# Moving the q and k transposes of an attention-plus-MLP kernel from TensorE to DMA, with a new order of the first batch

## The chip, the cores and the metric

The kernel runs on one NeuronCore of one Trainium2 chip. The metric is the device time of one execution in microseconds (us), as the median of several executions. The profile is one traced execution, and its span runs from the first instruction to the last, about 2 us less than the timed figure.

Engines are named as in the profile: PE is TensorE, PEld its weight loads, DVE is VectorE, ACT is ScalarE, POOL is GpSimd and SP is SyncE. "SPq" is the sequencer of SP while it issues DMAs. SP does nothing else here, and it works through its instructions in program order.

## The reference

Attention with a forget gate, then a two-layer MLP. Cut to what matters:

```python
# q, k, v: (8, 8, 576, 64) f32; f: (8, 8, 576) f32; w_in: (512, 2048); w_out: (2048, 512)
scores = matmul(q, k^T) / 8 + cum[..., :, None] - cum[..., None, :]     # cum = cumsum(log f)
scores = where(causal, -1e9, scores)                                     # strictly above the diagonal
attn   = softmax(scores)
x = matmul(attn, v).transpose(0, 2, 1, 3).reshape(8 * 576, 512)
h = x @ w_in
out = (h * sigmoid(h)) @ w_out                                           # (4608, 512) f32
```

## The kernel before

The work is cut into 32 *units*. A unit is a pair of heads (two times 64 columns fill 128 partitions), four units make a batch. For the scores, q and k are needed with the head dimension on the partitions. They come from memory with the sequence on the partitions, so each unit transposes nine blocks of 128 x 128: four of q, four of k, and one that holds the 64-row tails of both.

The parts that the change touches, with cuts marked:

```python
def load_qk(n):            # four DMAs of 128 KB on SP, q and k, four buffers each
    ...
def cast_qk(n, engs):      # f32 -> bf16, qkb, two buffers; POOL in the steady stage
    ...
def transposes(n):
    b, p = divmod(n, NP)
    src = qbf.pop(n)
    tp = psc.tile([P, 2048], BF16, name="tp", tag="sc")                  # PSUM
    for i in range(2):
        for c in range(NM):                                              # NM = 4
            o = i * (S + ST) + c * P
            nc.tensor.transpose(tp[:, o : o + P], src[:, i, c, :], ident_bf[:, :])
    nc.tensor.transpose(tp[:, SM : SM + P], tbf[b][:, p * P : (p + 1) * P], ident_bf[:, :])
    t = qktp.tile([P, QKW], BF16, name="qkT", tag="qkT")                 # two buffers
    nc.vector.tensor_copy(out=t[:, :], in_=tp[:, 0:QKW])                 # PSUM -> SBUF on DVE
    qkT[n] = t
```

`scores(n, c)` computes a quarter of a unit's scores from `qkT` on PE and their exponentials on ACT. `den(n // 2)` makes the denominators of two units. `rec_part` inverts them on DVE and then issues eight small DMAs on SP that spread the reciprocals over the partitions (`rb`). `num(n)` multiplies by v, with `vp` being v times the gate's weights, made on POOL. It then multiplies by `rb` into `xT`, the input of the MLP.

The MLP is cut into 288 *chunks* of four matmuls, either of the first layer (`hp`) or of the second (`po`). `fill(k)` puts up to k chunks that are ready into PE's program, between the attention's matmuls. What isn't put in earlier is done after the last unit.

```python
cast_qk(0, (nc.vector, nc.gpsimd)); cast_tails(0); transposes(0)
for n in range(NU):
    b, p = divmod(n, NP)
    scores(n, 0); scores(n, 1); fill(1)
    if n + 1 < NU: cast_qk(n + 1, (nc.gpsimd, nc.gpsimd))
    if n + 4 < NU: load_qk(n + 4)
    if n == 2:                                    # v of the first batch, then w_in, on POOL
        for c in range(NM + 1): convert_v(0, c)
        for i in range(WQ): load_w_in(i)
    ...                                           # w_out at unit 5; next batch's v: loads at p == 0,
    ...                                           # products at p == 2 and 3
    fill(1)
    scores(n, 2); scores(n, 3)
    fill(2 if n % 2 == 0 else 1)
    if n + 1 < NU: transposes(n + 1)
    fill(2)
    if n % 2 == 1:
        den(n // 2); rec_part(n // 2, 0); fill(2); rec_part(n // 2, 1); fill(1)
    elif n >= 2:
        num(n - 2); num(n - 1); fill(2); finished(n - 1)
fill(12); num(NU - 2); fill(2); num(NU - 1); finished(NU - 1)
while fill(1): pass
```

The softmax here doesn't subtract the row's maximum and nothing guards it: scores larger than these inputs give would overflow.

## Time and profile before

Three executions gave a median of 421.75 us, from 420.9 to 421.83.

| stage (profiled run, 418.7 us) | PE busy | PE clock | DMA share |
|---|---|---|---|
| 20 to 45 us (start) | 7.0 of 25 us | 0.71 | 1.13 |
| 45 to 66 us (start) | 10.5 of 21 us | 0.58 | 0.92 |
| 142 to 310 us (units 12 to 27) | 159.0 of 168 us | 1.00 | 0.60 |

The DMA share counts whole every packet that starts in the stretch, so it can pass 1. PE clock is the granted share of full speed.

The page of the kernel before comes first. The rows of tenths give the busy share in 40 equal slices of the span, and PEclk is the granted clock in tenths.

```profile
span 418.7 us, 8037 instructions
...
PE 359.0 (86%) x3109; PEld 176.8 (42%) x3109; DVE 249.9 (60%) x406; ACT 213.2 (51%) x328; POOL 95.9 (23%) x140
...
PE   1650456989998999899989998999899989999996
...
PEclk9995565999999999999999999999999999999999
DMA  8999699761696179617861696169614021300111
...
q1 hardware_dynamic: 124944, 47.36, 50.1%
...
PE 50%; DVE 17%; SPq 11%; ACT 9%; DMA 6%; issue 5%; POOL 1%; ACTq 0%; DVEq 0%; POOLq 0%
...
L224 DVE COPY qkT<-tp 128x1152 bf16<-128x1152 bf16 x32 | 24.0, 750 | 4.2 <-PE tp L220 4.1
L219 PE MATMUL tp<-ident_bf,qkb 128*128 128x128 bf16 x256 | 21.9, 235 | 3.8 <-ACT u L254 2.9
```

PE is busy for 80% or more from slice 8 on (the last slice apart). Before that the DMA engines are busy for 60% to over 90%. The last two lines are the groups that the change removes: 288 PE transposes (256 here, 32 on the next source line) and 32 copies on DVE. The line of PE and DVE shares is the chain of waits that ended last.

The order in time of PE (start, duration, line, operation; in brackets the idle time before it and what ended it):

```profile
45.53 0.52 PE L247 MATMUL sc<-qkT 64*128 64x400 bf16 x2 [14.71 <-DVE xT L334]
...
65.32 0.52 PE L247 MATMUL sc<-qkT 64*128 64x400 bf16 x2 [5.30 <-DVE xT L334]
...
67.26 1.04 PE L352 MATMUL hp<-xT,w_in_bf 128*128 128x512 bf16 x2
...
156.20 0.61 PE L219 MATMUL tp<-ident_bf,qkb 128*128 128x128 bf16 x8 [0.20 <-ACT u L254]
156.65 0.22 PE L220 MATMUL tp<-ident_bf,qkt 128*128 128x128 bf16 x1
156.70 1.89 PE L352 MATMUL hp<-xT,w_in_bf 128*128 128x512 bf16 x8
```

Two things are read here. At the start PE stands still for 14.71 us before unit 3, until `xT` has its `rb`. In the steady stage nine transposes take 0.50 us of PE, from 156.20 to 156.70.

What held `rb` back is in the order of SP's issues:

```profile
15.69 1.15 SPq L112 DMA_DIRECT2D vf_129<-in_v_dram  x1
...
26.20 5.90 SPq L112 DMA_DIRECT2D vf_226<-in_v_dram  x1
32.16 4.12 SPq L77 DMA_DIRECT2D qf<-in_q_dram  x2
36.32 3.90 SPq L77 DMA_DIRECT2D kf<-in_k_dram  x2
40.33 5.02 SPq L312 DMA_DIRECT2D rb<-rec  x8
```

The first batch's v loads were all issued by 16.8 us. The `rb` of units 0 and 1 came at 40.33, behind loads of later units.

### The profile page before, as it was taken

The page shows a single profiled execution, that of the slowest core. Times are in us where ns is not written, and L with a number is a line of the kernel's source. Part 1 is how long each engine was busy: PE and PEld are TensorE (multiplying, and loading weights), DVE is VectorE, ACT ScalarE, POOL GpSimd, SP SyncE. Part 2 cuts the span into 40 slices and gives each one's busy share as a digit, 9 for nine tenths or more (in the row PEclk, how much of TensorE's full clock was granted, in tenths as well). Part 3 has the DMA queues.
Part 4 walks back from the last instruction along what each step waited for, and adds up shares of the span by engine and source line. Part 5 has one row for each costly group of instructions (what it writes and reads, how often), then busy time and mean ns, then how long its engine had stood idle before and what let it go on. Part 6 is the DMA issues. An engine that isn't in the chain of part 4 may idle for free.

```text
span 418.7 us, 8037 instructions
## 1 busy us (share of the span) xinstructions
PE 359.0 (86%) x3109; PEld 176.8 (42%) x3109; DVE 249.9 (60%) x406; ACT 213.2 (51%) x328; POOL 95.9 (23%) x140
## 2 busy tenths in 40 slices
PE   1650456989998999899989998999899989999996
PEld 1430232434543454345434444444444444444442
DVE  3670354976497649764976397549754964574410
ACT  3530334845484558455845484548454852463421
POOL 3682330601171116011601161116111000000000
PEclk9995565999999999999999999999999999999999
DMA  8999699761696179617861696169614021300111
GB/s 171 217 208 201 154 157 235 120 145 43 167 202 144 42 178 194 145 43 182 188 143 45 156 207 151 34 154 218 150 34 126 8 52 50 108 2 26 50 52 75
DMA packets 129206, 52.06 MB, mean 124 GB/s; under 512 B 116304, under 2 KB 120400, under 8 KB 129168
## 3 DMA queue, kind: packets, MB, share of 16 engines
q1 hardware_dynamic: 124944, 47.36, 50.1%
q0 software_dynamic: 4224, 4.19, 6.2%
q8 instruction: 24, 0.39, 0.4%
q14 instruction: 14, 0.11, 0.1%
HBM read 36.85 MB, written 9.44 MB: 111 GB/s over the span
## 4 chain that ended last, share of the span: by engine, by line
PE 50%; DVE 17%; SPq 11%; ACT 9%; DMA 6%; issue 5%; POOL 1%; ACTq 0%; DVEq 0%; POOLq 0%
PE po L379 26%; PE hp L352 14%; DVE gt L361 7%; DVE rec L304 6%; ACT u L254 6%; SPq L77 4%; SPq L312 4%; PE nm L325 3%; PE sc L247 3%; PE dn L290 2%; PE tp L219 2%; ACT th L360 2%; DMA out_dram<-osb 2%; SPq L112 1%; DVE u L261 1%
## 5 line engine op out<-in xcount | busy, mean ns | idle before, releaser
L352 PE MATMUL hp<-xT,w_in_bf 128*128 128x512 bf16 x576 | 137.6, 383 | 0.1
L379 PE MATMUL po<-w_out_bf,gt 128*128 128x512 bf16 x576 | 134.5, 380 | 0.0
L254 ACT ACTIVATE u<-sc 128x800 bf16<-128x800 f32 x128 | 101.2, 847 | 53.9 <-PE sc L247 43.9
L360 ACT ACTIVATE th<-hp 128x512 bf16<-128x512 f32 x144 | 85.0, 611 | 57.5 <-PE hp L352 53.0
L361 DVE SCALAR_TENSOR_TENSOR gt<-th,hp 128x512 bf16<-128x512 bf16 x144 | 94.1, 676 | 24.4 <-ACT th L360 23.7
L352 PEld LDWEIGHTS <-w_in_bf 128*128 128x128 bf16 x576 | 52.5, 98 | 60.9 <-issue 5.9
L379 PEld LDWEIGHTS <-gt 128*128 128x128 bf16 x576 | 52.7, 98 | 60.0 <-issue 2.0
L261 DVE TENSOR_TENSOR u<-u,mask 128x256 bf16<-128x256 bf16 x128 | 42.4, 346 | 57.7 <-ACT u L254 57.4
L247 PE MATMUL sc<-qkT 64*128 64x176 bf16 (+5 forms) x512 | 40.0, 269 | 36.2 <-DVE xT L334 20.0
L304 DVE RECIPROCAL rec<-rec 128x288 f32<-128x288 f32 x32 | 61.1, 1934 | 15.7 <-ACT rec L298 15.7
L388 ACT ACTIVATE osb<-po 128x512 f32<-128x512 f32 x36 | 21.5, 597 | 74.6 <-PE po L379 55.6
L96 POOL CAST qkb<-qf 128x512 bf16<-128x512 f32 x31 | 19.9, 643 | 142.2 <-PE tp L220 79.0
L334 DVE TENSOR_TENSOR xT<-nm,rb 128x576 bf16<-128x576 f32 x32 | 23.6, 753 | 43.5 <-DMA rb<-rec 26.7
L247 PEld LDWEIGHTS <-qkT 64*128 64x128 bf16 x512 | 20.3, 99 | 67.4 <-issue 63.0
L325 PE MATMUL nm<-u,vp 128*64 128x64 bf16 (+4 forms) x576 | 28.4, 250 | 8.4 <-DVE qkT L224 8.4
L325 PEld LDWEIGHTS <-vp 128*64 128x64 bf16 x576 | 21.0, 114 | 20.4 <-issue 15.9
L224 DVE COPY qkT<-tp 128x1152 bf16<-128x1152 bf16 x32 | 24.0, 750 | 4.2 <-PE tp L220 4.1
L219 PE MATMUL tp<-ident_bf,qkb 128*128 128x128 bf16 x256 | 21.9, 235 | 3.8 <-ACT u L254 2.9
L219 PEld LDWEIGHTS <-qkb 128*128 128x128 bf16 x256 | 18.8, 105 | 12.0 <-issue 5.2
L96 POOL CAST qkb<-kf 128x512 bf16<-128x512 f32 x32 | 20.1, 627 | 4.8 <-DMA kf<-in_k_dram 4.8
L103 POOL CAST qkt<-qktf 128x512 bf16<-128x512 f32 x8 | 4.9, 616 | 58.4 <-DMA qktf<-in_k_dram 58.4
L298 ACT ACTIVATE rec<-dn 128x576 f32<-128x576 f32 x16 | 10.4, 651 | 13.1 <-PE dn L290 12.9
(73 smaller groups left out, 112.7 us busy)
## 6 DMA issues: line engine op xcount, KB each, us to landing
rb<-rec SPq DMA_DIRECT2D x128, 72.0 KB, 2.0
out_dram<-osb SPq DMA_DIRECT2D x36, 256.0 KB, 2.3
qf<-in_q_dram SPq DMA_DIRECT2D x64, 128.0 KB, 3.1
kf<-in_k_dram SPq DMA_DIRECT2D x64, 128.0 KB, 3.0
w_in_bf<-in_moe_w_in_dram POOLq DMA_DIRECT2D x4, 512.0 KB, 11.1
w_out_bf<-in_moe_w_out_dram POOLq DMA_DIRECT2D x4, 512.0 KB, 9.9
qktf<-in_q_dram SPq DMA_DIRECT2D x8, 128.0 KB, 3.2
qktf<-in_k_dram SPq DMA_DIRECT2D x8, 128.0 KB, 3.5
```

Of the source, the lines that this page charges most:

```text
L96: engs[i].tensor_copy(out=t2[:, i, :, :], in_=t[:, :, :, :].rearrange("p c h d -> p c (h d)"))
L219: nc.tensor.transpose(tp[:, o : o + P], src[:, i, c, :], ident_bf[:, :])
L224: nc.vector.tensor_copy(out=t[:, :], in_=tp[:, 0:QKW])
L247: nc.tensor.matmul(sc[:, i, lo - c * CW : hi - c * CW], lhsT=t[r, k_off(kb) : k_off(kb) + P], rhs=t[r, q0 : q0 + hi - lo], start=True, sto ...
L254: nc.scalar.activation(out=u[:, :, c * CW : (c + 1) * CW], in_=sc[:, :, 0:CW], func=ACT.Exp, scale=scale)
L261: nc.vector.tensor_tensor(out=x, in0=x, in1=mask[:, None, :].to_broadcast([P, 2, P]), op=ALU.mult)
L304: nc.vector.reciprocal(out=rec[:, r], in_=rec[:, r])
L325: nc.tensor.matmul(nm[i * D : (i + 1) * D, q0:q1], lhsT=vp[:, kb, 2 * p + i, :], rhs=u_part(n, i, kb, q0, q1), start=(kb == 0), stop=(kb = ...
L352: nc.tensor.matmul(hp[:, :], lhsT=w_in_bf[:, cc, fc * P : (fc + 1) * P], rhs=xT[:, cc, t0 : t0 + TG], start=(cc == 0), stop=(cc == NCC - 1),)
L360: nc.scalar.activation(out=th[:, :], in_=hp[:, :], func=ACT.Tanh, scale=0.5)
L361: nc.vector.scalar_tensor_tensor(out=gt[:, fc, :], in0=th[:, :], scalar=1.0, in1=hp[:, :], op0=ALU.add, op1=ALU.mult,)
L379: nc.tensor.matmul(po[:, :], lhsT=gt[:, fc, tb * P : (tb + 1) * P], rhs=w_out_bf[:, fc, :], start=(fc == 0), stop=(fc == NFC - 1),)
```

## The change

The intent is to take 32 times nine transposes off PE and the copies off DVE. One DMA transpose per unit now goes from SBUF to SBUF, issued by SP. The first batch is put in a new order, so that PE doesn't wait for `rb` in units 0 to 3. The diff, cut to its core:

```diff
-    qktp ... bufs=2      rbp ... bufs=3      qf, kf ... bufs=4      qktf ... (1)
+    qktp ... bufs=3      rbp ... bufs=4      qf, kf ... bufs=5      qktf ... bufs=2
     def cast_qk(n, engs):                 # the tails now go into the same tile, nine blocks wide
...
     def transposes(n):
-        ...  nine nc.tensor.transpose into PSUM, one nc.vector.tensor_copy
+        t = qktp.tile([P, NX, P], BF16, name="qkT", tag="qkT")
+        nc.sync.dma_start_transpose(
+            out=t[:, :, :], in_=qbf.pop(n)[:, :, :].rearrange("p x c -> p (x c)")
+        )
+        qkT[n] = t[:, :, :].rearrange("p x c -> p (x c)")
...
-            can2 = c < 16 * (a // 16)
+            can2 = c < 16 * (a // 16) and a >= 32          # second layer only after 32 first-layer chunks
...
     transposes(0)
+    for n in range(1, NP):
+        load_qk(n + 1)
+        cast_qk(n, (nc.gpsimd, nc.gpsimd))
+        if n == NP - 1:
+            for c in range(NM + 1): load_v(0, c)
+        transposes(n)
+    for i in range(WQ): load_w_in(i)
+    for c in range(NM + 1): convert_v(0, c)
+    load_tails(1); load_qk(NP + 1)
     # unit n:
         scores(n, 0); scores(n, 1); fill(1)
-        cast_qk(n + 1), load_qk(n + 4)
+        cast_qk(n + 2), load_qk(n + 5)
-        v(b + 1): loads at p == 0, products at p == 2, 3      w_out at unit 5
+        v: loads at p == 2, products at p == 0, 1 of its own batch (b > 0)   w_out at unit 6
-        fill(1)
+        fill(1 if n >= 2 * NP else 0)                         # fewer fills in units 4 to 7
         scores(n, 2); scores(n, 3)
-        fill(2 if n % 2 == 0 else 1); transposes(n + 1); fill(2)
+        fill(4 - n % 2 if n >= 2 * NP else 1)
         den, rec_part (odd n)  /  num(n - 2), num(n - 1) (even n)
+        # num(0) to num(3) all at the end of unit 3, then fill(4)
+        if n + 2 < NU and n + 2 >= NP:
+            transposes(n + 2)                                 # at the end of the unit
+        if n + 5 < NU and 1 <= n < NP: load_qk(n + 5)
+        if n == NP - 1: load_v(1, ...)
```

Below, T(n) is the DMA transpose of unit n.

More of the change, by code (lines that the diff above doesn't have):

```diff
@@ L42 @@
     NM = SM // P
+    NX = 2 * NM + 1
     assert D == 64 and S == 576 and DM == H * D and NP == NCC
@@ L51 @@
     vpool = ctx.enter_context(tc.tile_pool(name="vpool", bufs=3))
-    qktp = ctx.enter_context(tc.tile_pool(name="qktp", bufs=2))
+    qktp = ctx.enter_context(tc.tile_pool(name="qktp", bufs=3))
     upool = ctx.enter_context(tc.tile_pool(name="upool", bufs=4))
     recp = ctx.enter_context(tc.tile_pool(name="recp", bufs=2))
-    rbp = ctx.enter_context(tc.tile_pool(name="rbp", bufs=3))
+    rbp = ctx.enter_context(tc.tile_pool(name="rbp", bufs=4))
     tpool = ctx.enter_context(tc.tile_pool(name="tpool", bufs=3))
@@ L67 @@
     qbf: dict[int, bass.AP] = {}
-    tbf: dict[int, bass.AP] = {}
     vbf: dict[int, bass.AP] = {}
@@ L74, in load_qk @@
         for name, src in (("qf", q), ("kf", k)):
-            t = stage.tile([P, NM, 2, D], FP32, name=name, tag=name, bufs=4)
+            t = stage.tile([P, NM, 2, D], FP32, name=name, tag=name, bufs=5)
             for i in range(2):
@@ L84, in load_tails @@
     def load_tails(b):
-        t = stage.tile([P, H, D], FP32, name="qktf", tag="qktf")
+        t = stage.tile([P, H, D], FP32, name="qktf", tag="qktf", bufs=2)
         for i, src in enumerate((q, k)):
@@ L93, in cast_qk @@
     def cast_qk(n, engs):
-        t2 = conv.tile([P, 2, NM, 2 * D], BF16, name="qkb", tag="qkb")
+        b, p = divmod(n, NP)
+        t2 = conv.tile([P, NX, 2 * D], BF16, name="qkb", tag="qkb")
         for i, t in enumerate(qst.pop(n)):
+            c0 = i * (NM + 1)
             engs[i].tensor_copy(
-                out=t2[:, i, :, :], in_=t[:, :, :, :].rearrange("p c h d -> p c (h d)")
-            )
+                out=t2[:, c0 : c0 + NM, :],
+                in_=t[:, :, :, :].rearrange("p c h d -> p c (h d)"),
+            )
+        nc.gpsimd.tensor_copy(
+            out=t2[:, NM, :],
+            in_=tst[b][:, 2 * p : 2 * p + 2, :].rearrange("s h d -> s (h d)"),
+        )
         qbf[n] = t2
-    def cast_tails(b):
-        t2 = conv.tile([P, H * D], BF16, name="qkt", tag="qkt")
-        nc.gpsimd.tensor_copy(out=t2[:, :], in_=tst.pop(b)[:, :, :].rearrange("s h d -> s (h d)"))
-        tbf[b] = t2
     def load_v(b, c):
@@ L120 @@
     load_tails(0)
-    for n in range(1, NP):
-        load_qk(n)
-    for c in range(NM + 1):
-        load_v(0, c)
+    load_qk(1)
     ident_bf = const.tile([P, P], BF16, name="ident_bf")
@@ L177 @@
     )
+    cast_qk(0, (nc.vector, nc.vector))
     nc.vector.tensor_copy(out=wexp[:, S : S + ST], in_=wexp[:, SM:S])
@@ L204, in convert_v @@
         )
-    QKW = 2 * S
     def k_off(kb):
@@ L212, in transposes @@
     def transposes(n):
-        b, p = divmod(n, NP)
-        src = qbf.pop(n)
-        tp = psc.tile([P, 2048], BF16, name="tp", tag="sc")
-        for i in range(2):
-            for c in range(NM):
-                o = i * (S + ST) + c * P
-                nc.tensor.transpose(tp[:, o : o + P], src[:, i, c, :], ident_bf[:, :])
-        nc.tensor.transpose(
-            tp[:, SM : SM + P], tbf[b][:, p * P : (p + 1) * P], ident_bf[:, :]
-        )
-        t = qktp.tile([P, QKW], BF16, name="qkT", tag="qkT")
-        nc.vector.tensor_copy(out=t[:, :], in_=tp[:, 0:QKW])
-        qkT[n] = t
+        t = qktp.tile([P, NX, P], BF16, name="qkT", tag="qkT")
+        nc.sync.dma_start_transpose(
+            out=t[:, :, :], in_=qbf.pop(n)[:, :, :].rearrange("p x c -> p (x c)")
+        )
+        qkT[n] = t[:, :, :].rearrange("p x c -> p (x c)")
     UO = [0]
@@ L411, in finished, with steady @@
             ready["g"] += 1
-    cast_qk(0, (nc.vector, nc.gpsimd))
-    cast_tails(0)
     transposes(0)
-    for n in range(NU):
+    for n in range(1, NP):
+        load_qk(n + 1)
+        cast_qk(n, (nc.gpsimd, nc.gpsimd))
+        if n == NP - 1:
+            for c in range(NM + 1):
+                load_v(0, c)
+        transposes(n)
+    for i in range(WQ):
+        load_w_in(i)
+    for c in range(NM + 1):
+        convert_v(0, c)
+    load_tails(1)
+    load_qk(NP + 1)
+    def steady(n):
         b, p = divmod(n, NP)
@@ L421 @@
         fill(1)
-        if n + 1 < NU:
-            cast_qk(n + 1, (nc.gpsimd, nc.gpsimd))
-        if n + 4 < NU:
-            load_qk(n + 4)
-        if n == 2:
-            for c in range(NM + 1):
-                convert_v(0, c)
-            for i in range(WQ):
-                load_w_in(i)
-        if n == 5:
+        if n + 2 < NU and n + 2 >= NP:
+            cast_qk(n + 2, (nc.gpsimd, nc.gpsimd))
+        if n + 5 < NU and n >= NP:
+            load_qk(n + 5)
+        if b + 1 < B:
+            if p == 0 and b > 0:
+                load_tails(b + 1)
+            if p == 2 and b > 0:
+                for c in range(NM + 1):
+                    load_v(b + 1, c)
+        if b > 0:
+            if p == 0:
+                for c in range(2):
+                    convert_v(b, c)
+            if p == 1:
+                for c in range(2, NM + 1):
+                    convert_v(b, c)
+        if n == NP + 2:
             for i in range(WQ):
                 load_w_out(i)
-        if b + 1 < B:
-            if p == 0:
-                load_tails(b + 1)
-                for c in range(NM + 1):
-                    load_v(b + 1, c)
-            if p == 2:
-                cast_tails(b + 1)
-                for c in range(2):
-                    convert_v(b + 1, c)
-            if p == 3:
-                for c in range(2, NM + 1):
-                    convert_v(b + 1, c)
-        fill(1)
+        fill(1 if n >= 2 * NP else 0)
         scores(n, 2)
         scores(n, 3)
-        fill(2 if n % 2 == 0 else 1)
-        if n + 1 < NU:
-            transposes(n + 1)
-        fill(2)
+        fill(4 - n % 2 if n >= 2 * NP else 1)
         if n % 2 == 1:
@@ L455 @@
             rec_part(n // 2, 0)
-            fill(2)
+            fill(2 if n >= 2 * NP else 1)
             rec_part(n // 2, 1)
-            fill(1)
-        elif n >= 2:
+            fill(1 if n >= 2 * NP else 0)
+            if n == NP - 1:
+                for m in range(NP):
+                    num(m)
+                finished(n)
+                fill(4)
+        elif n >= 2 and n != 2 and n != NP:
             num(n - 2)
             num(n - 1)
-            fill(2)
+            fill(2 if n >= 2 * NP else 1)
             finished(n - 1)
+        if n + 2 < NU and n + 2 >= NP:
+            transposes(n + 2)
+        if n + 5 < NU and 1 <= n < NP:
+            load_qk(n + 5)
+        if n == NP - 1:
+            for c in range(NM + 1):
+                load_v(1, c)
+    for n in range(NU):
+        steady(n)
     fill(12)
```

## The prediction

> **What bounds the kernel now.** Three stages, from the timeline and the busy table by stretches (unit = head pair).
>
> - Start, 0 to 100 us (units 0 to 7). Not TensorE: PE is busy 7.0 of 25 us in 20-45 at clock 0.71, 10.5 of 21 us in 45-66; the DMA share is 1.13 and 0.92. PE waits 14.7 us before 45.5 for xT, xT for rb, whose eight issues started only at 40.3, behind v and q/k issues of up to 5.9 us on the SP queue. A second such wait, 5.3 us, ends at 65.3. The first hp matmul starts at 67.3.
> - Steady, 100 to 352 us: 10.5 us per unit, PE bound (153-195: busy 39.9 of 42 us). In the chain of waits eight MLP matmuls take 1.73 us (216 ns each), so eight fills of four are 6.9 us; scores, num, den about 1.8; transposes 0.50 (156.20 to 156.70); about 1.2 are bubbles.
> - Tail, 352 to 419 us: MLP at 216 ns per matmul.
>
> **Removed.** 288 PE transposes, 0.50 us x 32 = 16 us of PE time, 12 us of it in the PE-bound stage. 32 qkT copies on DVE (24.0 us, 750 ns each); the waits show PE num 8.4 us and PE scores 4.5 us behind them: I expect 2 to 4 us from that.
>
> **Added.** 32 DMA transposes of 295 KB. Estimate: the DMA page's q1 has 124,944 packets taking 50.1% of 16 engines' span, 27 ns each; 1152 rows of 256 B over 16 engines are 1.9 us. The Trainium skill ("DMA: Bandwidth & Descriptors", Latency and other measured facts) gives DMA transposes 261 GB/s, so 1.1 us; this trace shows none. Steady DMA: 0.60 x 10.5 + 2 = 8.3 of 9.9 us per unit, tight, not binding. SP's issues at 0.5-0.6 us each are about 6.5 us per unit; I guess 2 us for a transpose, so 8.5. Two units of lead and a third qkT buffer hide its latency.
>
> **Moved.** w_in comes right after the first units' loads; num(0..3) wait for unit 3, so scores 0 to 3 don't stall on rb; v(1) and w_out come later. Unit 4 should start near 42 us, the first hp at 38-45 instead of 67. Units 4 to 7 do 3 fills each, at 7 to 9 us (DMA, SP, DVE bound), so unit 8 starts near 74 instead of 100. By then 16 fills are done instead of 24: 8 x 0.86 = 7 us return in the tail. Net start gain about 19 us.
>
> **Sum.** 74 + 24 x 9.85 (236) + tail 67 + 7 = 384 us span, about 386 us timed; range 373 to 412. Faster by over 2%: 0.82; within 2%: 0.09; slower: 0.09.
>
> **Right if** PE waits before 60 us shrink by over half; first hp near 40 us; unit pitch 9.6-10.0 us; transposes land in 2-5 us; scores wait little on qkT. **Wrong if** the pitch stays 10.5 (the transposes were in bubbles), unit 8 starts after 85, or the tail grows by over 10 us.
>
> **What would make it wrong.** A transpose that holds SP over 4 us, or moves under 100 GB/s: SP is in order, so rb, outputs and loads queue behind it and a unit takes 11 us or more. A backlog of loads at the start could delay transposes 0 to 3. A PE idle for longer at the start may run at a lower clock.

## The result and the profile after

The changed kernel took **441.02 us** (median of four executions, 438.02 to 441.99) against **421.36 us** for the kernel before in the same rounds. The ratio is 1.0455, with a 95% interval of 1.0401 to 1.0508: slower. Ratios here are the mean time of one kernel's fast runs over that of the other's of the same rounds, so they are not quite the ratio of the quoted medians.

The page after, in the lines that answer to those above:

```profile
span 436.2 us, 7419 instructions
...
PE 336.6 (77%) x2774; PEld 158.4 (36%) x2821; DVE 235.0 (54%) x375; ACT 213.2 (49%) x328; POOL 97.9 (22%) x163
...
PE   0511728608298899788988997898899899999996
...
PEclk9999859957789999999999999999999999999999
DMA  6999769899544987697598839894941413001011
...
q1 hardware_dynamic: 162832, 56.80, 61.2%
...
PE 42%; SPq 27%; DMA 18%; ACT 5%; issue 4%; DVE 2%; POOL 1%; POOLq 0%; DVEq 0%; ACTq 0%
```

PE lost 22.4 us of busy time, of which about 16 us are the transposes. A few per cent of its matmul records are missing from this trace (560 and 545 of 576 in the two MLP groups), so the rest isn't to be read. The span grew by 17.5 us although PE has less to do: PE now waits. In the chain of waits SP's sequencer and the DMAs went from 17% to 45%.

The order in time of PE after:

```profile
41.82 0.85 PE L238 MATMUL sc<-qkT 64*128 64x400 bf16 x6 [18.34 <-DMA qkT<-qkb]
...
53.97 0.63 PE L343 MATMUL hp<-xT,w_in_bf 128*128 128x512 bf16 x1 [0.33 <-issue]
60.72 0.59 PE L343 MATMUL hp<-xT,w_in_bf 128*128 128x512 bf16 x1 [6.12 <-DVE xT L325]
...
67.38 0.52 PE L238 MATMUL sc<-qkT 64*128 64x400 bf16 x6
...
97.67 0.85 PE L238 MATMUL sc<-qkT 64*128 64x400 bf16 x6 [13.85 <-DMA qkT<-qkb]
...
182.32 0.51 PE L238 MATMUL sc<-qkT 64*128 64x400 bf16 x6 [2.13 <-DMA qkT<-qkb]
...
192.37 0.52 PE L238 MATMUL sc<-qkT 64*128 64x400 bf16 x6 [1.05 <-DMA qkT<-qkb]
```

These are the starts of units 3 (41.82), 4 (67.38), 7 (97.67), 15 and 16. The old wait before unit 3 is gone in name but not in size: 18.34 us for a transposed q and k, where it was 14.71 us for `xT`. Unit 7 has a new one of 13.85 us. Units far into the steady stage wait 1 to 2 us each. The table of waits gives the sum (engine, line, what it waited for, us in total, times, longest):

```profile
PE sc L238 <- DMA qkT<-qkb: 63.5, 18, 18.3
```

SP's issues at the start and in the steady stage, after, show why:

```profile
20.66 0.51 SPq L115 DMA_DIRECT2D vf_198<-in_v_dram  x1
...
23.56 7.18 SPq L115 DMA_DIRECT2D vf_201<-in_v_dram  x1
30.79 4.43 SPq L115 DMA_DIRECT2D vf_202<-in_v_dram  x1
35.33 4.24 SPq L213 DMA_TRANSPOSE qkT<-qkb  x1
...
43.31 5.04 SPq L303 DMA_DIRECT2D rb<-rec  x8
...
50.80 1.61 SPq L213 DMA_TRANSPOSE qkT<-qkb  x1
...
55.84 4.96 SPq L303 DMA_DIRECT2D rb<-rec  x8
```

```profile
173.05 5.01 SPq L303 DMA_DIRECT2D rb<-rec  x8
178.18 2.16 SPq L213 DMA_TRANSPOSE qkT<-qkb  x1
...
188.15 1.82 SPq L213 DMA_TRANSPOSE qkT<-qkb  x1
```

At the start SP is never free from 19.56 to 62.17 us. T(3) stands behind the five v loads, the first `rb` group behind T(3) and six loads, T(4) behind four more loads, and the second `rb` group behind T(4) and another four. Each is needed by PE. In the steady stage T(15) is issued at the moment when the eight `rb` issues end, and the scores of unit 15 start 2.0 us after its issue ends. T(16) stands behind five v loads. So the transposes that were meant to be two units ahead are finished just in time or late.

The view of the transpose's own line gives issue time (min/median/max in ns) and the time to landing:

```profile
L213 SPq DMA_TRANSPOSE qkT<-qkb x32: 1256/1595/4237, 8.6 to 342.1; - x32
...
DMA to landing us min/median/max: 3.2/3.9/8.2
```

Where the time went, as start of units in us, with the number of MLP chunks that PE had done by then:

| | unit 3 | unit 4 | unit 6 | unit 8 | unit 12 | unit 28 | end |
|---|---|---|---|---|---|---|---|
| before | 45.5 | 52.4 (0) | 78.3 (8) | 100.2 (24) | 142.1 (56) | 310.3 (184) | 418.7 |
| after | 41.8 | 67.4 (4) | 77.8 (9) | 106.4 (15) | 151.8 (40) | 315.5 (168) | 436.2 |

At unit 12 the changed kernel is 9.7 us late and owes 16 chunks. A chunk is four matmuls of 216 ns, 0.864 us, so the debt is 13.8 us: together 23.5 us. From unit 12 to 28 it gains 4.5 us. I call "lateness plus debt" the **work-adjusted delay** and use it below. It compares kernels that do their MLP work at different times.

### The profile page after: what moved, and what is told of

The parts are those of the page before. It is cut to its first block, busy times and chain, and to the rows that moved or that the text cites. A ratio compares the mean times of both kernels' runs of the same rounds, so it can differ in the third digit from the quotient of the medians.

```text
span 436.2 us, 7419 instructions
## 1 busy us (share of the span) xinstructions
PE 336.6 (77%) x2774; PEld 158.4 (36%) x2821; DVE 235.0 (54%) x375; ACT 213.2 (49%) x328; POOL 97.9 (22%) x163
## 3 DMA queue, kind: packets, MB, share of 16 engines
q1 hardware_dynamic: 162832, 56.80, 61.2%
## 4 chain that ended last, share of the span: by engine, by line
PE 42%; SPq 27%; DMA 18%; ACT 5%; issue 4%; DVE 2%; POOL 1%; POOLq 0%; DVEq 0%; ACTq 0%
PE hp L343 19%; PE po L370 18%; SPq L303 11%; DMA qkT<-qkb 11%; SPq L77 6%; SPq L115 5%; SPq L213 4%; DMA vf_199<-in_v_dram 3%; ACT u L245 3%; PE sc L238 3%; DMA rb<-rec 2%; PE nm L316 2%; ACT th L351 2%; PE dn L281 1%; DMA vf_3622<-in_v_dram 1%
## 5 line engine op out<-in xcount | busy, mean ns | idle before, releaser
L343 PE MATMUL hp<-xT,w_in_bf 128*128 128x512 bf16 x560 | 141.0, 390 | 10.4 <-DVE xT L325 8.0
L370 PE MATMUL po<-w_out_bf,gt 128*128 128x512 bf16 x545 | 132.5, 379 | 3.3 <-issue 2.5
L245 ACT ACTIVATE u<-sc 128x800 bf16<-128x800 f32 x128 | 100.0, 841 | 68.1 <-PE sc L238 67.8
L252 DVE TENSOR_TENSOR u<-u,mask 128x256 bf16<-128x256 bf16 x128 | 53.2, 431 | 74.2 <-ACT u L245 73.1
L238 PE MATMUL sc<-qkT 64*128 64x176 bf16 (+5 forms) x512 | 38.9, 269 | 70.2 <-DMA qkT<-qkb 63.5
L370 PEld LDWEIGHTS <-gt 128*128 128x128 bf16 x576 | 53.8, 98 | 64.2 <-issue 2.6
L316 PEld LDWEIGHTS <-vp 128*64 128x64 bf16 x576 | 20.3, 115 | 14.9 <-issue 10.0
L281 PE MATMUL dn<-u,w_bf 128*32 128x64 bf16 (+4 forms) x576 | 15.9, 256 | 1.3 <-DVE u L252 0.9
L281 PEld LDWEIGHTS <-w_bf 128*32 128x32 bf16 x576 | 10.6, 101 | 11.5 <-issue 7.1
L103 POOL CAST qkb<-qktf 128x128 bf16<-128x128 f32 x32 | 9.7, 303 | 5.5 <-DMA qktf<-in_k_dram 5.5
L257 DVE TENSOR_TENSOR u<-u,mask_t 128x128 bf16<-128x128 bf16 x32 | 7.6, 238 | 0.0
## 6 DMA issues: line engine op xcount, KB each, us to landing
w_in_bf<-in_moe_w_in_dram POOLq DMA_DIRECT2D x4, 512.0 KB, 11.8
```

The source lines that it names most:

```text
L238: nc.tensor.matmul(sc[:, i, lo - c * CW : hi - c * CW], lhsT=t[r, k_off(kb) : k_off(kb) + P], rhs=t[r, q0 : q0 + hi - lo], start=True, sto ...
L245: nc.scalar.activation(out=u[:, :, c * CW : (c + 1) * CW], in_=sc[:, :, 0:CW], func=ACT.Exp, scale=scale)
L252: nc.vector.tensor_tensor(out=x, in0=x, in1=mask[:, None, :].to_broadcast([P, 2, P]), op=ALU.mult)
L281: nc.tensor.matmul(dn[32 * j : 32 * j + 32, q0:q1], lhsT=w_bf[:, kb, bh : bh + 1].to_broadcast([P, 32]), rhs=u_part(n, i, kb, q0, q1), sta ...
L316: nc.tensor.matmul(nm[i * D : (i + 1) * D, q0:q1], lhsT=vp[:, kb, 2 * p + i, :], rhs=u_part(n, i, kb, q0, q1), start=(kb == 0), stop=(kb = ...
L343: nc.tensor.matmul(hp[:, :], lhsT=w_in_bf[:, cc, fc * P : (fc + 1) * P], rhs=xT[:, cc, t0 : t0 + TG], start=(cc == 0), stop=(cc == NCC - 1),)
```

## The experiments

My theory after reading the traces: (a) the place of T in SP's in-order queue costs the steady stage; (b) the start is bound by DMA traffic and by SP, so neither a new order nor DMA transposes can shorten it, and the transposes add to it; (c) the fewer fills only move work into the tail. The rivals: each transpose is simply too costly (its bytes, or SP's time); or the order of v and w_in at the start is the whole fault; or the fills are. Every run below gave correct results.

| run | median us | ratio to before [95%] | unit 8 at us (chunks) | delay at unit 12 | us per unit, 12 to 28 |
|---|---|---|---|---|---|
| before | 420.7 to 421.4 | 1 | 100.2 (24) | 0 | 10.51 |
| the change | 441.02 | 1.0455 [1.0401, 1.0508] | 106.4 (15) | +23.5 | 10.23 |
| e1_early_issue | 426.09 | 1.0135 [1.0104, 1.0165] | 100.2 (15) | +16.0 | 9.88 |
| e2_start_order | 442.11 | 1.0514 [1.0477, 1.0551] | 106.5 (15) | +22.7 | 10.53 |
| e4_transposes_only | 424.27 | 1.0078 [1.0044, 1.0112] | 113.5 (24) | +12.9 | 10.15 |
| e5_reorder_only | 437.88 | 1.0412 [1.0380, 1.0445] | 93.5 (15) | +11.8 | 10.81 |
| e6_old_fills | 423.37 | 1.0033 [1.0001, 1.0064] | 113.7 (32) | +12.1 | 10.07 |
| e7_hybrid | 409.57 | 0.9712 [0.9671, 0.9753] | 98.6 (24) | -4.2 | 10.20 |
| e7b_hybrid_v_late | **405.37** | 0.9624 [0.9599, 0.9650] | 98.7 (24) | -2.9 | 9.90 |
| e8_double_transpose | 431.68 | 1.0234 [1.0211, 1.0256] | | | 11.18 |
| e9_tiny_issues | 436.17 | 1.0360 [1.0314, 1.0407] | | | 11.11 |
| e10_plain_copy_bytes | 426.08 | 1.0133 [1.0087, 1.0178] | | | 10.76 |
| e16_new_start_pe | 411.15 | 0.9758 [0.9715, 0.9802] | 102.9 (32) | +0.7 | 9.80 |
| e18_hybrid_k_on_act | 406.43 | 0.9667 [0.9641, 0.9693] | | | 9.75 |
| e19_loads_on_act | 490.07 | 1.1658 [1.1634, 1.1682] | | | 12.10 |
| e20_w_in_after_v | 437.16 | 1.0404 [1.0363, 1.0445] | 102.7 (15) | +19.0 | 10.33 |
| e21_best_w_in_after_v | 406.20 | 0.9662 [0.9626, 0.9697] | 100.3 (32) | -1.9 | 9.78 |

The profiled execution of e8 fell in the slow state (437.08 us; its other three were 430 to 432), so its 11.18 may be a little high, and so may its row in the table of SP times below.

### e1: issue each transpose right behind its casts

```diff
 # the changed kernel, unit n
         cast_qk(n + 2, (nc.gpsimd, nc.gpsimd))
+        transposes(n + 2)
...
-        if n + 2 < NU and n + 2 >= NP:
-            transposes(n + 2)           # was at the end of the unit
```

> The changed kernel, with each DMA transpose of unit n+2 issued right behind its casts at the start of unit n, instead of at the end of unit n behind the rb issues (odd units) or the v loads (even units). Theory A (late issue: the in-order SP queue puts the transpose behind rb and loads, so the lead of two units shrinks to 2 us): scores stop waiting for qkT after 110 us (under 5 us in all, against about 45), pitch of units 8 to 31 falls from 10.39 to about 9.85 us, time 422 to 428 us. Theory B (the transposes' DMA traffic itself slows everything): landings stay slow, pitch stays at 10.3 or more, time 434 or more.

It gained 14.9 us on the change. The waits of the scores for their transposed operands fell from 63.5 us in 18 places to three, and the pitch (us per unit) fell from 10.23 to 9.88, close to the 9.85 that I had predicted for the change. The expectation was for units 8 to 31, where it fell less, from 10.39 to 10.08. The table of waits of e1:

```profile
PE sc L238 <- DMA qkT<-qkb: 22.9, 3, 17.9
```

In SP's order in e1, T(16) is now ahead of the v loads and no longer behind them, and the scores of unit 16 start 9.1 us after its issue ended (it was 2.4 us). (T is L213.)

```profile
172.57 1.35 SPq L213 DMA_TRANSPOSE qkT<-qkb  x1
...
176.26 4.55 SPq L115 DMA_DIRECT2D vf<-in_v_dram  x5
```

So part (a) stands: the same transposes, with the same bytes and about the same SP time (8.34 and 8.56 us per unit), cost 15 us more in the place that the change gave them. Half of that lies before unit 12, where the delay falls by 7.5 us. The three waits that are left all end by 40.9 us. After 110 us there is none, where the change had 24.3 us of them (not the 45 that I wrote in the expectation). The kernel is still slightly slower than before.

### e2: T(3) ahead of the first batch's v loads

```diff
     for n in range(1, NP):
         load_qk(n + 1); cast_qk(n, ...)
-        if n == NP - 1:
-            for c in range(NM + 1): load_v(0, c)
         transposes(n)
+    for c in range(NM + 1): load_v(0, c)
     for i in range(WQ): load_w_in(i)
```

> The changed kernel, with the fourth transpose issued before the five loads of v of the first batch, instead of behind them. Theory A: the 18.3 us wait of TensorE before unit 3 (ends at 41.8) shrinks to under 3 us, unit 8 starts 5 to 15 us earlier than 106.4, time 425 to 434. Rival (the start is limited by the bytes of v and w_in, in whatever order): xT of unit 3 is still not ready before 60 us, unit 8 starts within 3 us of 106.4, time 436 to 441.

PE's order in time in e2, units 3 and 4:

```profile
33.28 0.85 PE L238 MATMUL sc<-qkT 64*128 64x400 bf16 x6 [10.11 <-DMA qkT<-qkb]
...
67.31 0.51 PE L238 MATMUL sc<-qkT 64*128 64x400 bf16 x6
```

Unit 3 came 8.5 us earlier, and unit 4 not at all (67.31 against 67.38). The five v issues still took SP from 22.15 to 39.16, and the `rb` group behind them started at 42.98 instead of 43.31. The rival was right here (its range for the time, 436 to 441, was missed by 1 us): T(3)'s long wait is the first thing one sees in the trace, but it isn't the one that ends last.

### e4: only the transposes swapped, in the order of before

```diff
 # the kernel before; transposes(n) is the DMA transpose, tails cast into the same tile
     cast_qk(0, ...); transposes(0)
+    cast_qk(1, ...); transposes(1)
...
-        cast_qk(n + 1, ...)                 # and transposes(n + 1) late in the unit
+        cast_qk(n + 2, ...)
+        transposes(n + 2)
```

> The kernel before with only its transposes swapped: DMA transposes two units ahead, issued right behind their casts; first batch, fills and load order as before. Theory A: pitch about 9.85 us in the steady stage, start within 5 us of before (unit 8 at 95 to 105), time 402 to 410. Theory B: pitch 10.3 or more, time 418 or more. Theory C (the reordering of the first batch and the fills alone make the change slow): this kernel is faster than before, as under A.

The first form of this, with T in the old place and one unit ahead, could not be run: its build stops with a deadlock. By the order of the program, a v load on SP waits for POOL's product of the batch before, that product stands behind a cast, the cast waits for a buffer that T frees, and T stands behind the v load on SP. So in this order the DMA transposes needed an earlier place.

As run, e4 is 0.8% slower than before, which is a miss: I had expected 402 to 410 us or, if the transposes were costly everywhere, 418 or more with a pitch of 10.3. In the steady stage it gains 0.36 us a unit. At the start the first scores begin at 21.1 instead of 11.1 us, because T(0) stands behind all the first loads on SP and is issued only at 16.9. By unit 12 it is 12.9 us late, at equal chunks. Of this, 7.0 us are left by unit 28.

### e5: only the reorder, transposes on TensorE

```diff
 # the changed kernel; transposes(n) as nine nc.tensor.transpose and a copy on DVE, in the change's place
-    qktp ... bufs=3     rbp ... bufs=4
+    qktp ... bufs=4     rbp ... bufs=3
```

> The changed kernel with its transposes back on TensorE and DVE (a fourth qkT buffer, one rb buffer less, both forced by order and space); all reordering kept. Theory A: pitch back at 10.4 to 10.5 us, start better than the changed kernel since no transpose stands in the SP queue (unit 8 at 85 to 98), tail as in the changed kernel, time 415 to 425. Theory C: unit 8 still at 103 or later, time 430 or more.

The reorder alone costs 4.1%. Here, too, my expectation failed: unit 8 came in the range of theory A, the time in that of theory C. It reaches unit 8 at 93.5 us, with 15 chunks instead of 24, so it isn't ahead, and at unit 12 it is 11.8 us behind after the debt is counted. Together with e4 this gives a small two-by-two table of the work-adjusted delay at unit 12:

| | TensorE transposes | DMA transposes |
|---|---|---|
| order of before | 0 | +12.9 (e4) |
| order of the change | +11.8 (e5) | +23.5 (the change) |

The two parts each cost about 12 us at the start. That they add up to the 23.5 us is partly luck, since the two entries hold delays that the change doesn't have. Unit 0 starts at 21.1 us in e4, where T(0) stands behind the first loads. In e5 it starts at 16.7 us, because PE's program has the transposes of units 0 to 3 ahead of unit 0's scores. In the change it starts at 12.1 us, in the kernel before at 11.1. A cleaner pair is e6 and e16 below. The pitch of e5, 10.81, is worse than that of before. Its PE transposes stand at the end of a unit, but v, the fills and the buffers differ too, so the cause of that isn't shown.

### e6: e1 with the fills of before

```diff
 # e1
-            can2 = c < 16 * (a // 16) and a >= 32
+            can2 = c < 16 * (a // 16)
-        if n == NP + 2:                     # w_out
+        if n == NP + 1:
...
-        fill(1 if n >= 2 * NP else 0) ...   # and the other four conditional fills
+        fill(1) ...                         # as many in units 4 to 7 as in later units
```

> The early-issue kernel, with the MLP schedule of before in units 4 to 7: eight fills per unit instead of three, no gate that holds the second matmul back until 32 first chunks are done, w_out at unit 5. Theory D (the tail carries eight more MLP chunks only because the new fills hold them back): unit 8 still starts near 100 us, but about 24 chunks are done there instead of 16, the tail shrinks by about 7 us, time 417 to 421 against 426. Rival (the start has no room for them: rb, w_out and the SP queue bound it, and a chunk put in there pushes unit 8 back by its own length): unit 8 starts 5 us or more later, time 424 or more.

By unit 8, 32 chunks were done instead of 15, but unit 8 then started at 113.7 instead of 100.2: 17 chunks are 14.7 us, and 13.5 us of them were paid at once. The net gain is 2.7 us. So the thin fills are hardly the fault: in units 4 to 7 the chunks found little idle time of PE to hide in.

### e7 and e7b: TensorE transposes up to unit 7, DMA transposes from unit 8

```diff
 # the kernel before; ND = 2 * NP = 8
     def transposes(n):
+        if n < ND:  nine nc.tensor.transpose, copy on DVE
+        else:       nc.sync.dma_start_transpose(...)
...
-        if n + 1 < NU: cast_qk(n + 1, ...)
+        if n + 1 < ND: cast_qk(n + 1, ...)
+        if ND <= n + 2 < NU:
+            cast_qk(n + 2, ...); transposes(n + 2)
 # e7b: besides, from the third batch on, v as in the change (loads at p == 2, products at p == 0 and 1)
```

> The kernel before, with TensorE transposes up to unit 7 and DMA transposes, issued behind their casts two units ahead, from unit 8 on. The start of before should stay as it is (unit 8 at 100 us, 24 chunks done), the pitch afterwards as in the transposes-only kernel, 10.10 us, or 9.9: time 408 to 413, ratio 0.97 to 0.98. If the transposes' DMA traffic cost something beyond the start, pitch 10.3 or more and time 416 or more.

> The same hybrid, with the v loads of the next batch moved to the batch's third unit and their products to the next batch's first two units (as the change has them), from batch 1 on. Pitch as in the early-issue kernel, 9.92 instead of 10.10: time 404 to 409, ratio 0.96 to 0.97. If the place of v does not matter, the same as the other hybrid within 1 us.

Both beat the kernel before, by 2.9% and 3.8%. e7b, at 405.37 us, is the fastest of all. Its start is that of before (unit 8 at 98.7 with 24 chunks) and its pitch is 9.90. So DMA transposes in the steady stage, in the right place, are a gain: 0.3 us a unit alone (10.51 to 10.20 in e7, 10.15 in e4), and 0.6 with v as late as in the change (9.90). No run has the late v with TensorE transposes in their old place, so how much of the other 0.3 is due to v by itself isn't shown. The change lost because the start, and the late place of T, came with it.

### e8, e9, e10: what a transpose costs the steady stage

e8 issues every T twice. e9 adds three tiny copies of 16 x 32 bytes on SP behind every T: SP time and hardly any bytes. e10 adds one plain copy of 295 KB in 256-byte rows: bytes and one issue.

```diff
 # e7b, behind the dma_start_transpose of unit n
+            nc.sync.dma_start_transpose(out=t2[:, :, :], in_=src...)                    # e8
+            for i in range(3): nc.sync.dma_start(out=t2[0:16, i, :], in_=src[0:16, i, 0:16])   # e9
+            nc.sync.dma_start(out=t2[:, :, 0:P], in_=src[:, :, :])                      # e10
```

> The hybrid with v late, with every DMA transpose issued twice, the second into a tile that nobody reads: 7 MB more of transposed data from unit 6 on. Theory A (the transposes cost nothing while they come early): pitch within 0.15 us of the single one, time within 4 us. Theory B (their DMA traffic and SP time are costly in themselves): pitch up by 0.5 us or more, time up by 12 us or more.

> The hybrid with v late, with three copies of 16 partitions by 32 bytes issued on SP after every DMA transpose: about 1.5 us more of SP issue time per unit, like a second transpose, and next to no bytes. The doubled transposes cost 1.09 us per transpose (431.7 against 405.4 us for 24). If that was the SP queue's time, this costs about the same: time 425 to 433. If it was the bytes on the DMA engines, time 404 to 410.

> The hybrid with v late, with one plain copy of the same 295 KB, in the same 1152 rows of 256 bytes, into a scratch tile after every DMA transpose: about 0.5 us more of SP time per unit, and the bytes of a second transpose. If the doubled transposes cost bytes on the DMA engines, time 422 to 433. If they cost SP time, about a third of it: 408 to 415.

The 24 extra transposes of e8 cost 26.3 us, 1.1 us each. e9 is the surprising one: 72 copies of half a kilobyte cost 30.8 us, even more than I had expected of SP's time (425 to 433 us). The packets' time on the DMA engines can't be the reason: q1's packets took 62.8% of 405.2 us in e7b and 58.5% of 434.2 us in e9, 254 us in both. The chain of waits that ended last, in e7b and then in e9, shows SP's sequencer in place of PE:

```profile
PE 58%; SPq 11%; DVE 10%; ACT 8%; DMA 6%; issue 5%; POOL 2%; DVEq 0%; ACTq 0%; POOLq 0%
```

```profile
PE 37%; SPq 34%; DMA 12%; issue 7%; POOL 4%; ACT 4%; DVE 2%; DVEq 0%; POOLq 0%; ACTq 0%
```

Summed from the traces, over units 12 to 27:

| us per unit | SP issuing | pitch | SP more than e7b | pitch more than e7b |
|---|---|---|---|---|
| before | 6.55 | 10.51 | | |
| the change | 8.34 | 10.23 | | |
| e7b | 8.59 | 9.90 | | |
| e8 | 10.09 | 11.18 | +1.50 | +1.28 |
| e9 | 10.16 | 11.11 | +1.57 | +1.21 |
| e10 | 9.74 | 10.76 | +1.15 | +0.86 |
| e18 | 7.71 | 9.75 | -0.88 | -0.15 |

Added SP time came out in the pitch at 75% to 85%, with many bytes or few. SP had little room left: its pauses of over 0.12 us between issues, in the same units, come to 0.68 us per unit in e7b, and to 0.36, 0.10 and 0.29 in e8, e9 and e10. PE's granted clock between 142 and 310 us was also a little lower in these three (0.95, 0.96 and 0.97 against 1.00 in e7b), and what that adds to the pitch isn't separated. My expectation for e10 had two ranges, one for each theory, and the result, 426.08, fell in the one for bytes. The trace doesn't separate the two. One more copy took 0.74 us of SP, and the q loads' issues grew from 0.62 to 0.85 us in mean beside the added traffic, so bytes cost here as well, at least partly by making SP's issues longer. The copies of e9 also use completion semaphores. SP's DMAs take eight of them in turn, so a DMA may have to wait for the landing of the one eight places earlier, and three extra copies shorten that distance. The trace removes this doubt for the steady stage: in units 12 to 27 of e9 the DMA eight places earlier had landed before each issue began, and no pause of SP ended with such a landing.

### e18: half of the q and k loads issued by ACT

```diff
 # e7b
-                nc.sync.dma_start(
+                (nc.scalar if n >= 2 * NP and name == "kf" else nc.sync).dma_start(
```

> The hybrid with v late, with the loads of k for units 8 and up issued from the ACT queue instead of SP: SP's issue time falls from 8.6 to about 7.5 us per unit, the bytes stay. If SP's issue time is what still holds the pitch at 9.90, the pitch falls to 9.6 to 9.75 and the time to 400 to 403. If TensorE and its own waits hold it, pitch within 0.1 us of 9.90, time 404 to 407.

SP issues 0.88 us less per unit and the pitch falls by only 0.15 us; the time is that of e7b within the intervals. The expectation came out split, the pitch in the range for SP and the time in that for TensorE. SP's time no longer pays back at 75% to 85% here, so in e7b (8.6 of 9.9 us) it is hardly the limit. PE is the likely one, busy for 157.0 of 168 us between 142 and 310 us, but the loads also took time on ACT's queue, so that isn't shown. One step more on SP, as in e9, makes SP the limit.

### e19: all later loads issued by ACT

```diff
 # the changed kernel: load_v, and load_qk from n = 2 on
-                nc.sync.dma_start(
+                nc.scalar.dma_start(
```

> The changed kernel as it is, with all loads of v and the loads of q and k from unit 2 on issued from the ACT queue: the same transposes at the same late place, the same bytes, but no load stands before a transpose or an rb in the SP queue. Theory (order and issue time of the SP queue make the start and the late transposes slow): the wait of 18.3 us before unit 3 shrinks to under 5 us, unit 4 starts before 60 us instead of 67.4, pitch of units 12 to 28 at 10.1 or less instead of 10.23, time 420 to 431. Rival (the DMA engines' load from v, w_in and the transposes): unit 4 at 65 or later, time 436 or more.

This was a miss: 490 us, 16.6% slower, and it says nothing about SP. ACT issues in order too, and it has the exponentials to do. In its order in time:

```profile
33.13 5.95 ACT L245 ACTIVATE u<-sc 128x800 bf16<-128x800 f32 x8 [25.86 <-DMA vf<-in_v_dram]
```

The exponentials stood behind loads for 25.86 us. A queue that is moved onto a busy engine moves its waits there as well.

### e16: the new order with the transposes on TensorE up to unit 7

```diff
 # e6; ND = 8; qktp bufs 4, rbp bufs 3
-        transposes(n + 2): DMA, right behind the casts, for all units
+        units below ND: nine nc.tensor.transpose at the end of unit n; from ND on as in e6
```

> The change's first-batch order and the fills of before in units 4 to 7, with TensorE transposes up to unit 7 and early-issued DMA transposes from unit 8 on. Against the old-fills kernel (423.4, the same but DMA transposes from unit 0) it shows what DMA transposes cost in the start alone: theory, 5 to 9 us, so 414 to 419. Against the hybrid with v late (405.4, first batch as before) it shows what the new order of the first batch costs alone: 8 to 13 us. Rival (the order is harmless once the fills are restored and no transpose stands in the SP queue): 404 to 409.

This is the cleanest pair for the start. e6 and e16 have the same order and the same fills, and differ in how, and from which place in the unit, the first eight units are transposed (and in the buffers that this needs). 423.4 us becomes 411.2 us, and the delay at unit 12 goes from +12.1 to +0.7. So eight DMA transposes at the start cost about 12 us, 1.5 us each (I expected 5 to 9 us in all). The remaining 5.8 us to e7b (expected: 8 to 13) go with the new order of the first batch. With TensorE transposes it puts those of units 0 to 3 ahead of unit 0's scores in PE's program, and unit 0 starts at 16.6 us instead of 11.0 (11.7 in e6).

### e20 and e21: w_in after the v products

```diff
 # the changed kernel (e20); e16 (e21)
+    for c in range(NM + 1): convert_v(0, c)
     for i in range(WQ): load_w_in(i)
-    for c in range(NM + 1): convert_v(0, c)
```

> The changed kernel with one swap: the four w_in transfers are issued on the Pool queue behind the products of the first batch's v, so they start only when v has landed. Theory (w_in's traffic stretches the v loads to 13 to 17 us, the SP queue stands still behind them, and the fourth transpose and both rb groups wait in it): v lands within 7 us, unit 3 starts before 30 us instead of 41.8, the first rb group is issued before 35 us instead of 43.3, unit 4 starts near 55 instead of 67.4, and time falls by 5 to 12 us to 429 to 436. Rival (the start is held by the bytes, whatever their order, or by what comes later, units 6 to 9): unit 4 within 4 us of 67.4, or time 438 or more.

> The same swap in the kernel with the change's first-batch order, TensorE transposes up to unit 7, the old fills and early DMA transposes from unit 8 on (411.2 us). If the swap helps the start as the theory says, 402 to 408, as good as or better than the hybrid with v late (405.4). If not, 409 to 414.

In the change, w_in's four loads are issued on POOL at 20.34 us, at the same time as the v loads on SP, which then take up to 16.9 us to land. In e20 the v loads land in about 5 us, and unit 3 starts at 29.5 us. But SP's order in e20 shows what is then beside w_in:

```profile
31.03 5.46 SPq L303 DMA_DIRECT2D rb<-rec  x8
...
41.63 7.54 SPq L213 DMA_TRANSPOSE qkT<-qkb  x1
...
51.56 4.96 SPq L303 DMA_DIRECT2D rb<-rec  x8
```

The first `rb` group comes 12.3 us earlier, T(4) is stuck for 7.54 us, until 49.17 us (the last of w_in's loads lands at 49.25), and the second `rb` group comes only 4.3 us earlier. Unit 4 starts at 64.3 instead of 67.4 and the whole gains 3.9 us. The standstill moved to the next DMA that met w_in. The rival, that the traffic costs its time in whatever order, was mostly right. In e21 the same swap gives 5.0 us, and the result equals e7b within the intervals. So the new order of the first batch, with TensorE transposes, the old fills and the later w_in, is as good as the old one, and not better.

## Why the prediction was wrong

**The failed step: "Unit 4 should start near 42 us, the first hp at 38-45 instead of 67."** Measured: 67.4 and 54.0 us. I read from the profile that the start is bound by DMA (share 1.13 and 0.92) and by SP's long issues, and then treated its waits as a matter of order alone. The same loads, four transposes and both `rb` groups must still go through one in-order queue and 16 full DMA engines. Taking the wait away in one place made it appear in the next: e2 freed unit 3 and not unit 4; e20 freed unit 3 and the first `rb`, and lost it at T(4) and the second `rb`. The prediction had named this risk ("A backlog of loads at the start could delay transposes 0 to 3") and put no time on it.

Of the 52 us between the predicted span (384 us) and the measured one (436.2 us), 32 us lie before unit 8, 13 us in units 8 to 31 and 7 us in the tail (with the end of unit 31 taken one mean pitch of 10.39 us after its start at 345.3).

**"Units 4 to 7 do 3 fills each, at 7 to 9 us ... unit 8 starts near 74."** Measured: 39 us for units 4 to 7, with unit 8 at 106.4. 19.9 us of that are unit 6, where T(7) came behind an `rb` group that landed slowly beside w_out's loads (issued on POOL at 78.9, landed from 84.7 to 96.7). SP waited 2.2 us for one of its landings, and T(7) then took 8.2 us to land. That is the DMA cost of the start a second time. e16 against e6 measures the share of the transposes: DMA transposes in the first eight units cost about 12 us. My estimate had them as free in the start.

**"8 x 0.86 = 7 us return in the tail."** At unit 8 the debt was 9 chunks, close to the 8 that I had, but from there to unit 10 only 9 were done, against 16 in the kernel before, so 16 were owed from unit 10 on: 13.8 us. The mechanism was right, and its size was about double. e6 shows that it matters little: with the old fills the chunks that are no longer owed are paid for at once, by a later unit 8.

**"Two units of lead and a third qkT buffer hide its latency."** This is the error in reading the diff. `transposes(n + 2)` stands at the end of unit n, behind `rb` on odd units and behind the v loads in some even ones, and SP runs late. The real lead was about 2 us from the end of the issue to the scores. e1 moved the call and took 14.9 us off.

**What was right.** Costs of one transpose: 1.9 us of all 16 DMA engines predicted; q1's share rose from 50.1% of 418.7 us to 61.2% of 436.2 us, 57 us or 1.8 us for each of 32. SP: 2 us guessed, 1.6 us measured; 8.5 us of SP per unit predicted, 8.34 measured. Landing in 2 to 5 us: median 3.9. The pitch: 9.85 us predicted, 10.23 measured, 9.88 with the early issue. So the gain forecast for the steady stage, 0.6 us a unit, is there once T is issued early; but the transposes alone gave 0.3 (e7), and the prediction had put it all down to them. It was the smaller term in my sum: 19 us of gain were booked at the start, where 23.5 us were lost.

**The whole way from the change to the best kernel**, in medians: 441.0; early issue, 426.1 (-14.9); old fills, 423.4 (-2.7); TensorE transposes in the first eight units, 411.2 (-12.2); order of the first batch as before, with the late v of e7b from the third batch, 405.4 (-5.8).

**What the skill's pages say of it.** The Trainium skill ("DMA: Bandwidth & Descriptors", Issuing engines are not separate DMA queues) says that the time a sequencer needs to issue a DMA "is usually small relative to the DMA itself". Here it was not so small: a copy of 512 bytes took 0.65 us of SP and 2.0 us to land (e9), a transpose 1.6 and 3.9 us. The issues of one queue also add up: SP was issuing for 8.34 to 8.59 of about 10 us, and in e9 it was the limit. The same page's Rules for kernel authors tell one to issue a DMA early and wait for it late. e1 agrees, with 14.9 us. And the skill's page "VectorE: DVE Perf Modes" (The three transpose paths) gives 390 ns on TensorE and 1309 ns by DMA for a block of 128 x 128 in bf16. Here a TensorE transpose has a mean of 235 ns as one instruction but nine of them held PE for 0.50 us only, and a DMA transpose of nine blocks took 3.9 us to land. The thing removed was cheap to begin with.

**What stays open.** How much of a transpose's 1.1 us in the steady stage (e8) is SP's time and how much its bytes was not fully separated: e9 speaks for SP, e10 for both. What held SP's long issues at the start (7.18 us for one v load) was not shown either. It was no completion semaphore: the one that this load waits for belongs to a transpose that had landed at 20.4 us, 3 us before the issue began. T(4)'s issue in e20, which ended with the landing of w_in, points to the DMA traffic.

## What to carry to other kernels

A start that is full of DMA traffic is not made shorter by sending more through it, and a new order of it mostly moves the wait: here w_in after the v products was worth 4 and 5 us (e20, e21), and no order tried made the kernel faster than the order of before did. Keep its transposes on an idle TensorE, and use DMA transposes only once the loads thin out. When work moves to an in-order queue, read where in that queue it lands and what stands ahead of it: the lead is the time between the issue and the use, not the number of units in an index. Sum the issue times of the queue per unit against the unit's length before adding to it, since small copies take about as much of it as large ones (0.65 us for 512 bytes, 0.74 us for 295 KB).

## What the Trainium skill lacked or had wrong

- "DMA: Bandwidth & Descriptors" (Issuing engines are not separate DMA queues) calls issue time usually small relative to the DMA. Here it was about a third of the time to landing, or more (0.65 of 2.0 us for 512 bytes, 1.6 of 3.9 us for a transpose). The passage doesn't say that the issues of one queue add up: SP issued for 8.59 of 9.90 us per unit in e7b, and 72 added copies of 512 bytes cost 30.8 us (e9).
- The same page (Latency and other measured facts) has a bandwidth for DMA transposes, 261 GB/s, measured with a non-contiguous middle dimension (a condition that the prediction left out). For the 295 KB of one unit that is 1.1 us, an estimate; the runs show 1.8 us of all 16 engines' time, 3.9 us to landing, and 1.6 us of the issuing sequencer. It has no issue time for a transpose on this chip.
- The same page (Issuing engines are not separate DMA queues) says that DMAs from all issuing engines run on the same 16 DMA engines and interleave, but no page gives a size for loads from POOL beside those from SP: beside w_in's loads from POOL, v loads from SP that otherwise landed in about 5 us took up to 16.9 us, and a transpose's issue grew from 1.6 us to 4.24 us (the change) and 7.54 us (e20).
- "VectorE: DVE Perf Modes" (The three transpose paths) compares single blocks. Nine TensorE transposes in a row took 0.50 us of PE here, 56 ns each, far from nine times its 390 ns.
